# A fused adaLN, long-convolution and SwiGLU kernel on Trainium2: the first block of rows laid out anew

## The chip, the cores and the metric

The kernel runs on one core of one Trainium2 chip (trn2). The metric is the device time in microseconds of one execution; three runs of the kernel before gave a median of 492.25 us (492.23 to 493.86). A separate, profiled execution gives the trace that is read below.

## The reference, cut to what matters

```python
mod = (silu(c) @ w_mod)            # six rows of 576: sa, ca, ga, sb, cb, gb
h = layernorm(q) * (1 + ca) + sa
k_shift[s] = sum over t = 0..3 of k[s - t] * shift_k[:, t]
kv = k_shift * v
y = irfft(rfft(kv padded) * rfft(ssm_k padded))[:2048] + kv * ssm_D
x = q + ga * (h * y)               # a causal long convolution along the 2048 rows, per column
h = layernorm(x) * (1 + cb) + sb
out = x + gb * ((silu(h @ w1) * (h @ w3)) @ w2)
```

There are 2048 rows of 576 columns, the filter ssm_k has 2048 taps for each column, and w1, w3 are 576 x 4608, w2 4608 x 576. All tensors are bf16.

## The kernel before, in words

The rows are cut into eight blocks of 256; partition p of a block's tile holds rows 2p and 2p + 1. The long convolution is done block by block through short Fourier transforms. A block's kv is multiplied by cosine and sine matrices (Fb) on TensorE, which gives its spectrum X; the filter's block of taps, with taps along the partitions (kT), is multiplied by Fk, which gives W, and sums of neighbouring W give V. A block's output spectrum z is the sum of products X[i] V[s - i], in a form with three real products for a complex one; sums and differences of z (real_parts, or for block 0 four instructions in first_block) go through the inverse matrices in Fb. The result is multiplied by hg, the normed and modulated row, and added to x. The second layer norm follows, its rows are turned so that columns lie along the partitions (h2T), and the modulation by cb and sb is applied there as a scale and a bias for each partition (cbcol, sbcol).

The feed-forward part runs over four groups of 512 rows (two blocks each). stream multiplies h2T by chunks of w1 and w3, 512 columns of each per chunk, fetched from memory by SP's queue into wst and into room of the spectra (load_w13); ACT applies silu and copies, DVE multiplies. down multiplies by w2. While group r is streamed, the blocks of group r + 1 are convolved on DVE and ACT, with some matmuls between the streamed ones (conv; conv_second for block 1, beside the first half of stream 0). Group 0 is special: stream(0) begins with the first 256 rows alone, six chunks, as soon as block 0 is turned, and the rows of block 1 follow.

**What sets the order.** All operations are recorded first. Those of setup, early_loads and first_block are fixed: each engine gets them in the order in which they are written. All later ones are put in order by a planner (plan, search): it estimates every operation's time (measure), starts with forty random variations of due times, simulates each and keeps the order with the shortest mean time. It does this at build time, so a change of the fixed part can change the order of all that follows. Every operation is emitted at one line of a helper, so the profile shows L208 for nearly all, and they are told apart by the tiles' names. TensorE's results go to four pairs of PSUM banks (ps), of which the stream uses two. [...]

**Block 0 as it is (first_block, line 1301).** ACT computes the wave matrices by Sin from integer angles (angles, whole_turns, waves; tiles named spectra in the trace, since they lie in that room). shift_taps (846) spreads the four shift taps over all partitions by K = 1 matmuls. load_kv (925) loads k with its three shifted rows beside each pair, five rows of 576 for each partition; kv_rows (1019) forms kv by one product of 6 x 576 and five instructions of 2 x 576 on DVE. load_k (945) loads the taps as they lie, columns along the partitions; k_rows (1052) turns them by ten transposes on TensorE and one copy on ACT. ssm_D is added to tap 0 by two small matmuls, two copies and an addition. cond and mod_piece (869, 882) form the six modulation rows, spread over all partitions, on TensorE; mod_columns (907) forms cb and sb as columns by 60 matmuls. quick_stats (1155) takes a layer norm's statistics on DVE, ln_sums (1130) takes them on ACT. turn_split and turned_split (1262, 1269) turn a half block by six transposes and five evacuations with scale and bias; block 1 is turned by turn_all (1451), ten evacuations' worth in five instructions on ACT.

## Time and profile before

| what | us |
|---|---|
| median of 3 runs (lowest, highest) | 492.25 (492.23, 493.86) |
| profiled execution, its own time | 492.58 |
| its span in the trace | 490.6 |
| PE busy in 0 to 50 us, in 50 to 491 us | 43.44 of 50, 432.34 of 441 |
| DVE busy in 0 to 50 us | 43.21 |
| first matmul of h2T with wst starts at | 33.86 |
| data moved by DMA in the first 60 us | 18.38 MB, 306 GB/s |

The profiled execution's own time is its span and 1.98 us around it. Engines are PE (TensorE), PEld (its weight loads, which overlap), DVE (VectorE), ACT (ScalarE), POOL (GpSimd) and SP (SyncE, which here issues nearly all transfers). A line of the timeline gives the start, the duration, the engine, the operation, the tile written and those read, the shape, how many such instructions were merged, and in brackets how long the engine was idle before and what ended that. The chain of waits is followed back from the last instruction, at each step to what released it. [...] its cost in a row of matmuls is the distance between starts.

### The profile page before, as it was taken

How to read it: one execution, taken by the hardware profiler on the slowest of the kernel's cores; microseconds unless marked ns; L12 is line 12 of the kernel's file. 1: busy time of each engine (PE TensorE's matmuls, PEld its weight loads, DVE VectorE, ACT ScalarE, POOL GpSimd, SP SyncE). 2: the span in 40 equal slices, each digit the busy share in tenths (PEclk: the TensorE clock that was granted, in tenths of full speed). 3: DMA queues.
4: the chain of work that ended last, by engine and by line, in shares of the span. 5: the costliest groups of instructions: out<-in, count | busy, mean ns of one | idle time of the engine just before them, and what ended most of it. 6: DMA issues, size and time to landing. Idle time of an engine off the chain costs nothing.

```text
span 490.6 us, 11215 instructions
## 1 busy us (share of the span) xinstructions
PE 475.8 (97%) x4711; PEld 299.0 (61%) x4712; DVE 338.8 (69%) x450; ACT 285.2 (58%) x559; POOL 28.7 (6%) x41
## 2 busy tenths in 40 slices
PE   6899989998999999999999999999999999999997
PEld 3579879665777444444777444444777444444775
DVE  7988978999995949989776999998941211121012
ACT  5668498855564576778750567887572455555000
POOL 3200000001200000020200000010010000000000
PEclk9999999999999999999999999999999999999999
DMA  8999854665599998469999899764666445360562
GB/s 285 335 341 310 228 159 116 193 203 168 145 199 322 296 322 280 149 189 363 268 275 306 296 271 342 264 181 121 187 169 166 120 139 183 109 207 25 144 170 73
DMA packets 112614, 105.78 MB, mean 216 GB/s; under 512 B 20211, under 2 KB 105140, under 8 KB 112564
## 3 DMA queue, kind: packets, MB, share of 16 engines
q1 hardware_dynamic: 112542, 105.05, 71.9%
q8 instruction: 37, 0.61, 0.5%
q14 instruction: 13, 0.11, 0.1%
q10 hardware_dynamic: 22, 0.01, 0.0%
HBM read 90.10 MB, written 9.44 MB: 203 GB/s over the span
## 4 chain that ended last, share of the span: by engine, by line
PE 85%; DMA 6%; DVE 5%; SPq 1%; ACT 1%; issue 1%; POOL 0%; DVEq 0%; ACTq 0%
PE ps L208 85%; DMA wst<-in_B_w_dram 5%; SPq L208 1%; DVE kv L208 1%; DMA kh<-in_A_k_dram 1%; DVE z L208 1%; DVE bnst L208 1%; DVE hg L208 1%; DVE spectra L208 1%; ACT h2T L208 0%; DMA p<-in_A_shift_k_dram 0%; DVE og L208 0%; DVE p L208 0%; DVE x L208 0%; DVE bnmv L208 0%
## 5 line engine op out<-in xcount | busy, mean ns | idle before, releaser
L208 PE MATMUL ps<-h2T,wst 64*128 64x512 bf16 (+1 forms) x2736 | 277.9, 354 | 0.4 <-DMA wst<-in_B_w_dram 0.3
L208 PEld LDWEIGHTS <-wst 64*128 64x128 bf16 x2736 | 136.6, 94 | 121.9 <-PE ps L208 2.0
L208 PE MATMUL ps<-wst,h 128*128 128x288 bf16 x1152 | 144.1, 286 | 2.3 <-DMA wst<-in_B_w_dram 1.2
L208 PEld LDWEIGHTS <-h 128*128 128x128 bf16 (+2 forms) x1212 | 115.6, 98 | 33.9 <-issue 3.1
L208 ACT ACTIVATE h<-ps 128x512 bf16<-128x512 f32 x144 | 86.4, 600 | 62.5 <-PE ps L208 62.1
L208 ACT CAST u<-ps 128x512 bf16<-128x512 f32 x146 | 84.8, 582 | 56.7 <-PE ps L208 55.6
L208 DVE TENSOR_TENSOR h<-h,u 128x1024 bf16<-128x1024 bf16 x72 | 49.6, 689 | 71.8 <-ACT h L208 42.1
L208 DVE TENSOR_TENSOR p<-spectra 128x3456 bf16<-128x3456 bf16 x28 | 54.7, 1954 | 2.2 <-DMA spectra<-Xd 1.3
L208 DVE TENSOR_TENSOR z<-z,p 128x3456 bf16<-128x3456 bf16 x28 | 54.7, 1953 | 0.3
L208 DVE TENSOR_TENSOR og<-ps,gbrow 128x576 bf16<-128x576 f32 (+1 forms) x18 | 12.4, 690 | 41.7 <-PE ps L208 40.8
L208 ACT ACTIVATE junk<-x 128x576 bf16<-128x576 bf16 x52 | 35.8, 688 | 6.7 <-DVE x L208 6.2
L208 POOL TENSOR_TENSOR lnr<-lnv,neghalf 128x2 f32<-128x2 f32 x13 | 18.7, 1438 | 298.1 <-DVE lnv L208 279.8
L208 DVE TENSOR_TENSOR spectra<-spectra 128x1152 bf16<-128x1152 bf16 (+1 forms) x35 | 25.7, 736 | 2.7 <-ACT spectra L208 2.4
L208 PEld LDWEIGHTS <-Fb 64*128 64x128 bf16 (+1 forms) x250 | 16.0, 95 | 12.2 <-issue 2.2
L208 DVE TENSOR_TENSOR z<-z 128x1152 bf16<-128x1152 bf16 (+1 forms) x30 | 21.1, 710 | 0.1
L208 ACT CAST spectra<-ps 128x576 bf16<-128x576 f32 x32 | 20.4, 652 | 1.0 <-PE ps L208 1.0
L208 ACT ACTIVATE h2row<-x,lnn,lnr 128x64 bf16<-128x64 bf16 (+1 forms) x24 | 13.9, 644 | 10.5 <-DVE lnn L208 7.6
L208 PE MATMUL ps<-kv,Fb 64*128 64x288 bf16 (+1 forms) x142 | 19.3, 283 | 0.1
L208 PE MATMUL ps<-h2T,spectra 64*128 64x256 bf16 x288 | 17.9, 269 | 1.1 <-ACT h2T L208 1.1
L208 DVE TENSOR_TENSOR kv<-kv,p 128x1152 bf16<-128x1152 bf16 x24 | 18.1, 753 | 0.2
L208 PE MATMUL ps<-kT,Fk 64*128 64x288 bf16 (+1 forms) x118 | 17.2, 284 | 0.7 <-ACT kT L208 0.5
L208 PEld LDWEIGHTS <-spectra 64*128 64x128 bf16 x288 | 15.3, 94 | 2.5 <-issue 1.7
(91 smaller groups left out, 262.1 us busy)
## 6 DMA issues: line engine op xcount, KB each, us to landing
wst<-in_B_w_dram SPq DMA_DIRECT2D x72, 512.0 KB, 5.5
wst<-in_B_w_dram SPq DMA_DIRECT2D x72, 288.0 KB, 3.3
kh<-in_A_k_dram SPq DMA_DIRECT2D x7, 720.0 KB, 6.6
wst<-in_B_w_dram SPq DMA_DIRECT2D x72, 64.0 KB, 3.5
spectra<-Xd SPq DMA_DIRECT2D x5, 864.0 KB, 6.1
spectra<-Vd SPq DMA_DIRECT2D x5, 864.0 KB, 6.3
Xd<-spectra SPq DMA_DIRECT2D x4, 864.0 KB, 5.8
Vd<-spectra SPq DMA_DIRECT2D x4, 864.0 KB, 5.9
```

The lines of the kernel that those rows point to most:

```text
L208: getattr(getattr(nc, self.engine), self.method)(*[_real(a) for a in self.args], **{k: _real(v) for k, v in self.kw.items()})
```

## The change

- **Shift taps and kv.** shift_k is loaded to four partitions, and four K = 1 matmul pairs spread it. k of block 0 is loaded once, without shifted rows; DVE forms the products of its rows with each of the four taps, and TensorE adds them up in PSUM with unit matrices shifted by 0, 1 or 2 partitions (views of one tile, moved). DVE multiplies the sum by v.
- **Filter taps of blocks 0 and 1** come through a transposing DMA straight into kT, whose partition p now holds taps p and p + 128; Fk gets other angles for it, with a second pair by a sign, and for blocks 2 on pair_waves computes the former Fk at the start of conv_second. ssm_D enters as a K = 1 term of W's matmuls.
- **Products.** The sums and differences of z for block 0 go into the inverse matrices (Fi, formed on POOL): 12 matmuls for a half block, not 8. V's first part is written straight from PSUM, one half of it by DVE.
- **Rows split.** Row half 0 takes its first statistics on DVE and half 1 on ACT; for the second layer norm it is the other way round. The modulation rows are evacuated by ACT and multiplied by ga in bf16 on DVE.
- **mod_columns** forms the rows by 20 matmuls, copies one partition of each, and turns them by 12 small matmuls.
- **Loads.** w_mod is loaded in five pieces (2, 1, 0, 4, 3); the first chunk of w1 and w3 follows directly.
- **Turning.** Both halves of block 0 are turned after both are normed; three of five evacuations are DVE's. Block 1 is turned in the same way, a half at a time, in outcome. The three warm-up matmuls at the end are dropped, and four are set before shift_taps; all use a tile of zeros as both operands.

The diff, cut; lines taken out of first_block, load_kv, load_k, k_rows and mod_columns stand in the kernel above.

```diff
+        self.angles(nc.vector, 1)
+        self.whole_turns(1)
+        nc.vector.tensor_single_scalar(coli[:, 6:7], coli[:, 6:7], 1, op=ALU.bitwise_and)
+        nc.vector.tensor_copy(self.acol[:, 4:7], coli[:, 4:7])
+        nc.vector.tensor_scalar(self.sign[:], self.acol[:, 6:7], -2.0, 1.0, op0=ALU.mult, op1=ALU.add)
...
+        nc.gpsimd.memset(self.moved[:, 0:2], 0.0)
+        nc.gpsimd.run(lambda: make_identity(self.tc.nc, self.ident), 900.0, (self.ident,))
...
+        self.shk_raw = self.prod.tile([P, D], BF16, name="shk_raw", tag="p")
+        nc.scalar.dma_start(self.shk_raw[0:P:32, :], self.shift_k.rearrange("(q d) j -> q (d j)", q=4))
+        nc.scalar.dma_start(self.drow, self.ssm_D.rearrange("(o n) -> o n", o=1))
+        self.k0 = self.ld.tile([P, 2, D], BF16, name="kh", tag="kh")
+        nc.sync.dma_start(self.k0[:], self.k[0:B, :].rearrange("(p c) d -> p c d", c=2))
+        self.load_taps(0)
+        nc.sync.dma_start(self.crow[:], self.c)
+        self.load_v(0)
+        self.load_mod(2)
+        self.load_mod_tail(0, 3)
+        self.load_x(0)
+        self.load_mod(1)
+        self.load_mod(0)
+        self.load_mod_tail(3, 2)
+        self.load_mod(4)
+        self.load_mod(3)
+        self.load_w13(0, 0)
...
+    def taps_waves(self):
+        self.wave(self.Fk[:, 0:2], self.ang[1][:], 1)
+        self.nc.gpsimd.tensor_scalar(self.Fk[:, 2:4], self.Fk[:, 0:2], self.sign[:, 0:1], 0.0,
+                                     op0=ALU.mult, op1=ALU.add)
...
+    def inverse_sums(self):
+        nc = self.nc
+        for lo, hi, at in ((0, 1, 0), (3, 5, 1)):
+            n = hi - lo
+            nc.gpsimd.tensor_add(self.Fi[:, at:at + n, 0], self.Fb[:, lo:hi, 0], self.Fb[:, lo:hi, 1])
+            nc.gpsimd.tensor_scalar(self.Fi[:, at:at + n, 1], self.Fb[:, lo:hi, 0], -1.0, 0.0,
+                                    op0=ALU.mult, op1=ALU.add)
+    def pair_waves(self):
+        nc = self.nc
+        row = self.lnp.tile([P, P], I32, name="b_row2", tag="junk")
+        ang = self.lnp.tile([P, 2, 2, P], I32, name="ang2", tag="y")
+        nc.gpsimd.iota(row[:], pattern=[[4, P]], base=1, channel_multiplier=0)
+        for x in range(2):
+            for cs in range(2):
+                nc.gpsimd.tensor_scalar(ang[:, x, cs], row[:], self.acol[:, 4 + x:5 + x],
+                                        512.0 * (1 - cs), op0=ALU.mult, op1=ALU.add)
+        nc.vector.tensor_single_scalar(ang[:], ang[:], 2047, op=ALU.bitwise_and)
+        self.wave(self.Fk[:, 0:2], ang[:], 1)
...
+        for q in range(4):
+            at = slice(32 * q, 32 * q + 1)
+                nc.tensor.matmul(ps[:, h, 0:H], self.one[at, :], self.shk_raw[at, h * H:(h + 1) * H],
+                                 start=True, stop=True)
+            src = ps[:, :, 0:H].rearrange("p h (d j) -> p j h d", j=4)
+            dst = self.shk[:, :, 144 * q:144 * (q + 1)].rearrange("p j (h d) -> p j h d", h=2)
+            if q % 2:
...
     def mod_columns(self):
         nc = self.nc
+        rows = self.kvp.tile([1, 2, D], BF16, name="rows", tag="Wo")
+        for i, m in enumerate((4, 3)):
+            p = self.mod_products(m)
+            nc.scalar.copy(rows[:, i, :].rearrange("p (h d) -> p h d", h=2), p[0:1])
+            yield
         ps = self.ps()
+        for i in range(2):
             for j in range(6):
                 lo = min(P * j, 512)
                 n = P if j < 4 else 64
+                out = ps[0:n, i, 4 * j:4 * j + 4] if j < 5 else ps[64:P, i, 16:20]
+                nc.tensor.matmul(out, rows[:, i, lo:lo + n], self.one[0:1, 0:4], start=True, stop=True)
+        nc.scalar.activation(self.cbcol[:], ps[:, 0, 0:20:4], ACT.Copy, bias=1.0)
+        nc.scalar.copy(self.sbcol[:], ps[:, 1, 0:20:4])
...
+    def load_taps(self, s):
+        if s < SPLIT:
+            self.kT = dst = self.kvp.tile([P, 2, D], BF16, name="kT", tag="kT")
         else:
+            dst = self.knat
+        self.nc.sync.dma_start_transpose(dst[:], self.ssm_k[:, B * s:B * (s + 1)])
...
+                ps = self.products([(basis[e][cc][:, cs], rhs[:, cc, :]) for cc in range(2)]
+                                   + [(basis[e][0][0:1, cs], x) for x in more if cs == 0])
+                out = dst(e, cs).rearrange("p (h d) -> p h d", h=2)
+                if more and e + cs == 0:
+                    nc.vector.tensor_copy(out, ps[:, :, 0:H])
+                else:
+                    nc.scalar.copy(out, ps[:, :, 0:H])
...
+            basis = [[self.Fk[:, 2 * e + a] for a in range(2)] for e in range(2)]
+            V = self.V[s] = self.spec.tile([P, 6, D], BF16, name="V", tag="V")
+            yield from self.forward(basis, self.kT,
+                                    lambda e, cs: V[:, 3 * e, :] if s + cs == 0 else W[:, 2 * e + cs, :],
+                                    [self.drow] if s == 0 else [])
...
+    def shifted_rows(self):
+        nc = self.nc
+        p = [self.prod.tile([P, 2, 2, D], BF16, name="p", tag="p"),
+             self.acc.tile([P, 2, 2, D], BF16, name="p2", tag="z1")]
+        for i in range(2):
+            nc.vector.tensor_mul(p[i][:], _ap(self.k0, 0, [[0, 2], [D, 2], [1, D]]),
+                                 _ap(self.shk, 2 * i * D, [[D, 2], [0, 2], [1, D]]))
+        yield
+        ps = [self.ps() for _ in range(2)]
+        for js in ((0, 1), (2, 3)):
+            for c in range(2):
+                for j in js:
+                    at = (c - j) % 2
+                    d = (j - c + at) // 2
+                    for h in range(2):
+                        nc.tensor.matmul(ps[c][:, h, 0:H], self.moved[:, 2 - d:2 - d + P],
+                                         p[j // 2][:, j % 2, at, h * H:(h + 1) * H], start=(j == 0), stop=(j == 3))
+            yield
+        self.kv = kv = self.kvp.tile([P, 2, D], BF16, name="kv", tag="kv")
+        for c in range(2):
+            nc.vector.tensor_mul(kv[:, c, :].rearrange("p (h d) -> p h d", h=2), ps[c][:, :, 0:H],
+                                 self.vt[:, c, :].rearrange("p (h d) -> p h d", h=2))
...
     def first_block(self):
+        blank = self.h2T[0][:, 0, :]
+        self.warm(4, blank)
         self.shift_taps()
         self.whole_turns(0)
+        self.taps_waves()
+        self.forward_waves()
         self.cond_silu()
+        self.inverse_waves()
+        self.warm(6, blank)
+        rows = self.shifted_rows()
+        next(rows)
+        spectrum = self.w_spectrum(0)
+        next(spectrum)
+        next(rows)
+        next(spectrum)
+        next(rows)
+        self.run_all(rows)
         self.cond()
+        self.run_all(spectrum)
+        self.load_taps(1)
+        mean, rstd = self.quick_stats(x1[:, 0, :], "l1")
+        nmr = self.small.tile([P, 1], F32, name="l1nm", tag="nmr2")
+        nc.gpsimd.tensor_mul(nmr[:], mean, rstd)
+        nc.gpsimd.tensor_single_scalar(nmr[:], nmr[:], -1.0, op=ALU.mult)
         self.run_all(self.x_spectrum(0))
+        self.inverse_sums()
         self.run_all(self.v_block(0))
         self.load_kv(1)
         self.load_x(1)
         self.load_w13(1, 1)
         self.load_gb()
         X, V = self.X[0], self.V[0]
         self.accs[0] = z = self.acc.tile([P, 6, D], BF16, name="z0", tag="z0")
+        self.hg[0] = hg = self.lnp.tile([P, 2, D], BF16, name="hg", tag="hg", bufs=2)
+        ssum, ssq = [self.small.tile([P, 1], F32, name="l1" + k, tag=t) for k, t in (("s", "ssum"), ("q", "ssq"))]
+        self.ln_sum(x1, 1, 0, ssum[:])
+        self.ln_sum(x1, 1, 1, ssq[:])
         self.mod_piece(2)
+        nc.vector.tensor_add(X[:, 0, :], X[:, 1, :], X[:, 2, :])
+        nc.vector.tensor_mul(z[:, 0:3, :], X[:, 0:3, :], V[:, 0:3, :])
+        var = self.ln_square(ssum)
+        nc.vector.tensor_add(X[:, 3, :], X[:, 4, :], X[:, 5, :])
+        r = self.ln_rest(ssq, var)
+        nc.scalar.activation(hg[:, 0, :], x1[:, 0, :], ACT.Identity, bias=nmr[:, 0:1], scale=rstd[:, 0:1])
+        nc.vector.tensor_mul(z[:, 3:6, :], X[:, 3:6, :], V[:, 3:6, :])
+        b = self.ln_bias(ssum, r)
+        self.mod_piece(1)
+        nc.scalar.activation(hg[:, 1, :], x1[:, 1, :], ACT.Identity, bias=b[:, 0:1], scale=r[:, 0:1])
         for cc in range(2):
+            nc.vector.tensor_mul(hg[:, cc, :], hg[:, cc, :], self.arow[:])
+        self.mod_piece(0)
+        nc.vector.tensor_add(hg[:], hg[:], _ap(self.brow, 0, [[0, 2], [1, D]]))
+        y = self.lnp.tile([P, 2, D], BF16, name="y", tag="y")
+        ps = []
+        for cc in range(2):
+            terms = []
+            for e in range(2):
+                i = cc * (e + 1)
+                terms += [(self.Fi[:, i, 0], z[:, 3 * e, :]),
+                          (self.Fb[:, i + 2 if i else 0, 1], z[:, 3 * e + 1, :]),
+                          (self.Fi[:, i, 1], z[:, 3 * e + 2, :])]
+            ps.append(self.products(terms))
+        nc.scalar.copy(y[:, 0, :].rearrange("p (h d) -> p h d", h=2), ps[0][:, :, 0:H])
+        nc.vector.tensor_mul(hg[:, 0, :], hg[:, 0, :], y[:, 0, :])
+        nc.vector.tensor_add(x1[:, 0, :], x1[:, 0, :], hg[:, 0, :])
         self.residual_row(0, 1, ps[1])
+        ssum, ssq = [self.small.tile([P, 1], F32, name="l2" + k, tag=t) for k, t in (("s", "ssum"), ("q", "ssq"))]
+        self.ln_sum(x1, 0, 0, ssum[:])
+        self.ln_sum(x1, 0, 1, ssq[:])
+        columns = self.mod_columns()
+        next(columns)
+        var = self.ln_square(ssum)
+        box = []
+        st = self.quick_stats(x1[:, 1, :], "l2", lambda: box.append(self.ln_rest(ssq, var)))
+        r = box.pop()
+        next(columns)
         spectrum = self.w_spectrum(1)
+        next(spectrum)
+        self.run_all(columns)
+        b = self.ln_bias(ssum, r)
+        nc.vector.tensor_scalar(self.h2row[:, 0, 0:D], x1[:, 0, :], r[:, 0:1], b[:, 0:1], op0=ALU.mult, op1=ALU.add)
+        self.normed(0, 1, *st)
+        for cc in range(2):
+            pt = self.turn_split(cc)
+            self.turned_split(pt, cc)
         self.run_all(spectrum)
         self.accs.pop(0)
...
                     yield 1.25
                 for cc in range(2):
                     self.normed(s, cc, *st[cc])
+                    self.turned_split(self.turn_split(cc), 2 * s + cc)
...
-        if s > 1:
-            hT = self.h2T[(s // 2) % 2]
-            for cc in range(2):
-                t = 2 * (s % 2) + cc
-                self.nc.sync.dma_start_transpose(hT[:, :, t * P:(t + 1) * P], self.h2row[:, cc, :])
-            return
-        pt = self.ps((P, 2, 1024), BF16)
-        with self.rec.together():
-            for cc in range(2):
-                self.turn(pt, cc)
-        self.turned(s, pt, 0, 2)
...
     def conv_second(self):
+        self.pair_waves()
```

## The prediction

> **What bounds the kernel now.** I read the page's totals first, then the chain of work that ended last, then the timeline of the first 75 us by engine, then the stretches table there.
>
> ```profile
> PE 475.8 (97%) x4711; PEld 299.0 (61%) x4712; DVE 338.8 (69%) x450; ACT 285.2 (58%) x559; POOL 28.7 (6%) x41
> ```
>
> TensorE is busy 475.8 of 490.6 us, so from the first streamed weights on the end can hardly move except by what PE is given to do. Block 0 is different: there the chain runs along VectorE.
>
> ```profile
> 6.76 1.96 DVE p L208
> 8.72 0.68 DVE kv L208
> ...
> 17.39 1.07 DVE z L208
> ...
> 28.47 0.34 DVE h2row L208
> ...
> 30.98 0.60 DVE h2T L208 x2
> ...
> 64.45 2.39 ACT h2T L208 x5
> ...
> 66.88 49.64 PE ps L208 x682
> ```
>
> From 6.7 to 31 us nearly every piece is one DVE instruction after another. So block 0's DVE list, and what ACT and PE hand it, sets when block 0's rows are turned and the stream of weights can begin:
>
> ```profile
> 32.30 0.60 DVE L208 TENSOR_SCALAR h2T<-ps,cbcol,sbcol 128x128 bf16<-128x128 bf16 x2 [0.73 <-PE ps L208]
> 32.77 1.37 PE L208 MATMUL ps<-wst,u 128*128 128x288 bf16 x9
> 33.86 0.39 PE L208 MATMUL ps<-h2T,wst 64*128 64x256 bf16 x2
> ```
>
> The last of h2T is written at 33.16 (ACT's three, 31.99 + 1.17); the first streamed matmul starts at 33.86, after the last piece of the modulation (mod_piece(5), 32.77). The second bound here is the DMA queue: from 4 to 44 us its share is 0.99 or more in every 2-us stretch. The second and third lines show block 1.
>
> ```profile
> 42.00:44.00 2.00, 2.00 (x40) 2.00 (x37) 1.48 (x3) 1.27 (x3) 0.41 (x1) 1.00 1.12 352
> 60.00:63.00 3.00, 2.91 (x48) 1.89 (x44) 2.54 (x10) 2.18 (x5) 1.37 (x2) 1.00 0.56 111
> 63.00:67.00 4.00, 2.81 (x33) 1.71 (x33) 3.93 (x5) 3.62 (x9) 0.00 (x0) 1.00 0.21 72
> ```
>
> (Columns: stretch, length, busy us of PE, PEld, DVE, ACT, POOL, clock, DMA share, GB/s.) In 63 to 67 us PE is idle 1.19 of 4.00: block 1's turned rows, five ACT instructions in series (2.39 in the chain).
>
> [...] six 512-column warm-ups at 5.66 took 2.72 (0.45 each); at 10.66 sixteen of 288 columns took 2.12 (0.133 each). [...] the trace has 688 ns for 576 elements and 2.27 us for four in a row. [...] the trace has only the 128-element angles (2.48 us for six).
>
> **The change, part by part.** I lay the new program order on each engine with durations from the rows before.
>
> *Start and taps.* DVE loses kh's memset (0.78) and takes h2T's from POOL (0.53 there): constants to 1.9, four angles (0.9), one whole_turns (0.43), three tiny ones, to 3.6. PE's four warm-ups now start at about 1.65 and end at 3.4. The shift taps' four copies of 576 replace three of 1024/256; at 1.2 ns an element (1.22 for 1024) 0.70 each on DVE, about 0.65 on ACT; q0, q2 end at 5.7 on DVE, q3 on ACT at 6.15. DVE: whole_turns(0), now 768 wide, 0.62 to 1.05, take 0.7: 6.4. ACT: Fk, Fb, silu and inverse waves follow, to 9.55; the sign product on POOL costs 0.41 to 1.0 and ends near 7.9, hidden (wanted at 11).
>
> *Row sums.* Removed from DVE: 1.96 + 0.75 + 3 x 0.76 + 0.76 = 5.8 us (6.76 to 12.56). Added: two products of 2304 elements, 1.96 x 2304/3456 = 1.31 each, so 6.4 to 9.0; a PSUM copy of the first tap spectrum 0.70; two PSUM products of 0.75. PE adds 16 shift matmuls, 16 x 0.133 = 2.1, of which only the last eight (from 9.4, to 10.45) lie between. kv ends at 11.6: **1.0 earlier**.
>
> *Taps by transposing DMA.* Removed: 10 transposes (1.27) and an ACT copy (1.12), once per block; the drow columns and their copies. Added: four K=1 matmuls (0.5, PE has room) and SP's issue of a transpose: the trace has 1.55 and 1.30 against 1.05 for the two loads. Landing is 3.3 after issue with the queue free at 60 us, so 4.5 at best here; I take 6.5, before W's first product at 7.0. SP's queue behind it (c, v, the w_mod pieces) slips 0.5; c is wanted first, at 7.9, and landed 3 to 4 us after issue before. The second transpose waits for kT's readers (12.1)[...].
>
> *Spectra and products.* PE: cond, the last two W products and x_spectrum end at 14.2. ACT's four copies of X (2.27) end at 15.4 (16.37 before). DVE: one quick_stats (1.16) instead of two (2.32), no V copy (0.39), and of z only two sums (0.45) and two products (1.06): four of 0.47 = 1.9 are gone, for 8 more PE matmuls (24 for 16, +1.1) and Fi on POOL (four small two- and one-input operations, 1.5 to 2.5, by 16.5, hidden until 18.4). DVE would end z at 17.6, but waits for x1's row-1 sums, now on ACT (2 x 0.82 after 15.4 = 17.1): z ends at **18.4** (21.9 before).
>
> *Gate.* ACT becomes the chain: ga 17.75, hg row 0 18.5, arow 19.1, hg row 1 19.85, brow 20.45. DVE after it: 0.46 + 0.76, hg ready 21.7. Inverse on PE 18.4 to 21.6, y on ACT 21.05. Row 0: 0.46 + 0.46 = 22.6; row 1: 0.75 + 0.46 = 23.85 (28.47 before): **4.6 earlier**.
>
> *Statistics, columns, turn.* ACT: row 0's sums 24.3, two one-row copies 25.5, W copy 26.1, cbcol and sbcol 26.5. DVE: both h2row by 26.45 (31.07 before). mod_columns falls from 60 matmuls (4.44) to 20 of 0.14 and 12 small: 3.7, in PE's wait from 21.6 to 26.1. Turning: per half three DVE (0.30) beside two ACT (0.39), so 26.6 to 28.4. The last 12 matmuls of W(1) (1.6), before in gaps at 28.09 and 29.57, now stand behind the transposes, 27.2 to 29.0, since PSUM pairs come free only at 27.5 and 28.4. **First streamed matmul 29.0**, 4.9 earlier than 33.86.
>
> *What is given back.* mod_piece(5), ten full matmuls (1.37 at 32.77), stood ahead of the stream; its weights landed near 31.8 by the landing marks, so it now lies inside the stream: +1.4. Gain 3.5.
>
> *Weights.* The third chunk's last half is issued at 30.05 and, at the 8.0 us to landing of such 512 KB pieces, is there at about 38; PE first used it at 40.98, 7.1 after the stream began. After: wanted at 29.0 + 1.4 + 7.1 = 37.5. Bytes ahead fall by 0.43 MB (k's shifted copy: 1.3 us at 335 GB/s), while two transposes in a full queue cost 0 to 1.3 more each (the queue fell to 168 and 133 GB/s around the one at 46.80): landing 36.7 to 39.3, a wait of 0 to 1.8; I take **+0.3**.
>
> *Block 1.* DVE is full from 33 to 44 and nearly so to 62, so block 1's h2row moves with it, -4.5, but pair_waves puts 0.43 (the 512-wide row) on DVE, 0.72 on ACT and 2.5 on POOL there. Turning takes 1.8 on DVE and ACT together for the ACT series of 2.4, half of it before row 1 is normed. DVE side: about 60.5; PE, with its own work, 60.3. PE's idle 1.2 shrinks to about 0.3: **-0.9**.
>
> *After that* the same program follows; its order is searched anew by the planner, which I count at nothing, +-1.5 (the weights' waits it left before: 0.68 at 144.78, 0.53 at 247.21, 0.27 at 442.52).
>
> Sum: -4.9 + 1.4 + 0.3 - 0.9 = -4.1. On the profiled execution (span 490.6, 1.98 around it, 492.58) that is 488.5; its time is 0.33 above the median shown, 492.25, against which I forecast 488.1.
>
> **Rivals.** *A: the taps land late.* PE takes in order, and W's first product stands ahead of the shift sums; if the transpose lands at 9 rather than 6.5, kv and all behind it slip 2.0, giving 490.1. For: the queue is full from 2 us on. Against: only k lies ahead of it. *B: DMA decides.* Transposes block the queue fully (2.7 instead of 1.4 us each) and the third and fourth chunks wait; the stream's start is worth only what DMA came earlier, +1.8, giving 489.9. Against: the bytes fell. *C: the gain is whole.* PE hides mod_piece(5) in its remaining waits (-1.0) and turning ends at 28.0 (-0.8): 486.3. *D: slower.* The order searched anew issues weights too late at the changes from stream to block: a piece issued only when PE asks for it costs its whole landing, 6.4 (the chain's piece at 436.07, which is covered now). It decides once more than 4.1 + 2.5 = 6.6 us are lost, so from the second such piece: 492.25 - 4.1 + 12.8 = 501. For: the chain holds four such landings, and the planner's start times all move. Against: PE waited only 0.27 to 0.68 at them, and the later program is the same.
>
> **How the numbers follow.** Forecast 0.50 (486.6 to 489.6); C 0.17; A 0.13; B 0.12; D 0.08. About 0.5% (2.5 us) is what a measurement tells from no change, so the line lies at 489.8. Faster: 0.48 + 0.17 + 0.06 + 0.06 = 0.77; within: 0.02 + 0.07 + 0.06 = 0.15; slower 0.08. The range leaves out D and the far tail of C: 485.6 to 491.0.
>
> **What would show it.** kv ends near 11.6 on DVE; z near 18.4; the chain from 15 to 21 runs on ACT, not DVE; both h2row by 26.5; first matmul of h2T with wst near 29; PE idle at block 1's turn below 0.5. Wrong if W's first product waits for the transposing DMA past 7.5, if PE waits for the third chunk by over 1 us, or if PE's idle after 70 us grows by more than 1.5.

## The result and the profile after

| | before | after |
|---|---|---|
| median (lowest, highest), 14 runs each | 492.49 (491.76, 494.69) | 495.03 (493.63, 497.47) |
| after to before, 95% interval | | 1.0047 [1.003, 1.0064] |
| profiled execution, its span | 490.6 | 492.9 |
| first matmul of h2T with wst | 33.86 | 32.24 |
| PE idle after 70 us | 3.40 | 5.53 |

The change made the kernel slower by 0.47%, where 0.8% faster was forecast. The totals and two rows of the groups, from the page of after (total, mean ns, then idle before it):

```profile
PE 478.3 (97%) x4685; PEld 296.7 (60%) x4685; DVE 337.0 (68%) x453; ACT 289.2 (59%) x564; POOL 41.7 (8%) x49
...
L208 POOL TENSOR_TENSOR lnr<-lnv,neghalf 128x2 f32<-128x2 f32 x13 | 24.5, 1886 | 296.7 <-DVE lnv L208 296.7
...
L208 PE MATMUL ps<-h2T,spectra 64*128 64x256 bf16 x288 | 17.7, 269 | 1.4 <-DVE h2T L208 1.0
```

PE has 26 matmuls fewer than before and is busy 2.5 us longer, 2.3 of that in the first 28 us (24.73 busy, 22.45 before), where much of its work runs at half clock. POOL is busy 13 us longer. The chain of waits in block 0 (start, length, what):

```profile
3.87 0.69 PE ps L208 x8
4.56 0.75 DVE shk L208
5.31 0.04 issue
5.35 5.99 PE ps L208 x28
11.36 1.42 DVE kv L208 x2
...
16.07 3.79 POOL Wo L208 x4
19.85 0.56 POOL rstd L208
20.43 0.17 DVE nmr L208
20.63 0.87 ACT hg L208
...
29.26 11.96 PE ps L208 x141
```

The long DVE pieces of before (p 1.96, z 1.07) are gone from it. In their place stand PE (6 us up to kv) and POOL: the tile Wo holds the new inverse matrices Fi. PE up to kv, from the timeline (moved holds the shifted unit matrices; p and z are the products with the four taps, the second pair of which lies in z's room):

```profile
5.35 2.72 PE L208 MATMUL ps<-h2T 128*128 128x512 bf16 x6 [0.80 <-DVE shk L208]
7.86 1.05 PE L208 MATMUL ps<-kT,Fk 128*128 128x288 bf16 x4
...
9.19 1.15 PE L208 MATMUL ps<-p,moved 128*128 128x288 bf16 x8
10.18 0.65 PE L208 MATMUL ps<-kT,Fk 128*128 128x288 bf16 x4
10.67 1.14 PE L208 MATMUL ps<-z,moved 128*128 128x288 bf16 x8
```

The six warm-ups and the four matmuls of W's first piece start 0.43 and 0.24 us apart; from 8.84 us on, matmuls of 288 columns start 0.12 apart, at full clock. (One such matmul lasts 0.28 in the trace, the last of the sixteen at 13.68, so what it costs in a row is read from the starts. The clock column of the profile reads 1.00 in these first microseconds all the same; half clock at the start is read from the starts.) The end of block 0 on PE:

```profile
26.62 0.37 PE L208 MATMUL ps<-one,Wo 1*128 1x4 bf16 x6 [0.22 <-DVE bnst L208]
27.15 0.37 PE L208 MATMUL ps<-one,Wo 1*128 1x4 bf16 x6 [0.16 <-ACT Wo L208]
27.63 1.24 PE L208 MATMUL ps<-moved,h2row 128*128 128x128 bf16 x12
29.26 3.04 PE L208 MATMUL ps<-kT,Fk 128*128 128x288 bf16 x12 [0.39 <-ACT h2T L208]
32.24 1.94 PE L208 MATMUL ps<-h2T,wst 64*128 64x256 bf16 x30
```

h2T was complete at 30.22, but W(1)'s last twelve matmuls stood ahead of the stream and took 3.04 us, 0.24 from start to start; at full clock such a matmul takes 0.12. The stretches (the last three columns are clock, DMA share, GB/s) say so, and show block 1's turn below:

```profile
28.00:30.00 2.00, 1.61 (x14) 0.98 (x13) 1.52 (x7) 1.51 (x4) 1.43 (x4) 0.78 1.09 388
30.00:32.00 2.00, 2.00 (x10) 1.15 (x8) 2.00 (x2) 1.26 (x2) 0.00 (x0) 0.50 1.09 366
32.00:34.00 2.00, 2.00 (x32) 1.51 (x32) 2.00 (x4) 1.65 (x5) 0.00 (x0) 0.86 1.09 378
...
60.00:63.00 3.00, 2.93 (x48) 1.96 (x42) 2.01 (x8) 1.55 (x3) 1.48 (x2) 1.00 0.88 352
63.00:67.00 4.00, 2.62 (x41) 2.30 (x42) 4.00 (x9) 3.94 (x11) 0.00 (x0) 1.00 0.43 88
```

In 28 to 34 us, (0.22 + 0.50 + 0.14) x 2 = 1.72 us of clock were lost. In 63 to 67 PE is idle 1.38 us, where before it was 1.19: the new turning did not shorten it.

Followed by the stream's n-th matmul, after leads by 1.62 us at the first, trails by 0.16 at the 288th (52 us), is about level (0.08 behind) at the 433rd (65 us), and trails by 2.5 at the last. So in this pair of profiles what block 0 gained is gone by 52 us, and the rest is lost late. In a second pair (e17 and e12 below, the same two kernels) it leads by 2.3, 0.6 and 0.7 at these places and trails by 1.0 at the last.

### The profile page after: what moved, and what is told of

It reads as the page before. It is cut to its first block, busy times and chain, and to the rows that moved or that the text cites. A ratio compares the mean times of both kernels' runs of the same rounds, so it can differ in the third digit from the quotient of the medians.

```text
span 492.9 us, 11167 instructions
## 1 busy us (share of the span) xinstructions
PE 478.3 (97%) x4685; PEld 296.7 (60%) x4685; DVE 337.0 (68%) x453; ACT 289.2 (59%) x564; POOL 41.7 (8%) x49
## 4 chain that ended last, share of the span: by engine, by line
PE 75%; DVE 11%; POOL 5%; DMA 4%; ACT 3%; issue 1%; SPq 0%; POOLq 0%; ACTq 0%; DVEq 0%
PE ps L208 75%; POOL lnr L208 3%; DVE z L208 3%; DMA wst<-in_B_w_dram 2%; DVE p L208 2%; ACT junk L208 1%; DVE hg L208 1%; DVE h L208 1%; DMA kT<-knat 1%; POOL Wo L208 1%; DVE x L208 1%; DVE kv L208 1%; DMA p<-in_A_shift_k_dram 1%; DVE bnst L208 1%; ACT h L208 0%
## 5 line engine op out<-in xcount | busy, mean ns | idle before, releaser
L208 PEld LDWEIGHTS <-wst 64*128 64x128 bf16 x2736 | 135.0, 94 | 123.7 <-PE ps L208 2.1
L208 PEld LDWEIGHTS <-h 128*128 128x128 bf16 x1152 | 112.4, 98 | 31.8 <-issue 3.4
L208 ACT ACTIVATE junk<-x 128x576 bf16<-128x576 bf16 x56 | 38.4, 686 | 19.1 <-DVE x L208 18.5
L208 POOL TENSOR_TENSOR lnr<-lnv,neghalf 128x2 f32<-128x2 f32 x13 | 24.5, 1886 | 296.7 <-DVE lnv L208 296.7
L208 PEld LDWEIGHTS <-Fb 64*128 64x128 bf16 (+1 forms) x234 | 14.8, 95 | 12.3 <-DVE z L208 3.5
L208 ACT ACTIVATE h2row<-x,lnn,lnr 128x576 bf16<-128x576 bf16 (+1 forms) x24 | 14.0, 644 | 12.8 <-DMA h2T<-h2row 9.7
L208 PE MATMUL ps<-kT,Fk 64*128 64x288 bf16 (+1 forms) x120 | 19.5, 304 | 1.5 <-DMA kT<-knat 1.1
L208 DVE TENSOR_TENSOR z<-z 128x1152 bf16<-128x1152 bf16 x26 | 19.5, 751 | 0.1
L208 PE MATMUL ps<-kv,Fb 64*128 64x288 bf16 (+1 forms) x134 | 17.9, 284 | 0.2
L208 DVE TENSOR_TENSOR z<-spectra 128x3456 bf16<-128x3456 bf16 (+1 forms) x9 | 15.9, 1763 | 0.0
```

What stands on the lines that cost most here:

```text
L208: getattr(getattr(nc, self.engine), self.method)(*[_real(a) for a in self.args], **{k: _real(v) for k, v in self.kw.items()})
```

## The experiments

**Theory.** (a) Block 0 gains 1.6 and not 4.9 because its new path runs on PE, which is at half clock up to 8.8 us and again from 29.1 to 32.5, and because POOL's Fi sums hold a power that DVE waits for (a power: POOL raises a layer norm's variance to -1/2). (b) The new order of the later part puts POOL's powers, z and loads where PE waits for them. **Rivals:** the weights decide, so the start of the stream is worth nothing; the later order as such costs the time; the clock falls by itself.

In all experiments but e12 and e17 the order of everything behind block 0 is the list that the planner gave for after, kept, except where an edit moves something. Ratios are to the kernel before run beside them (35 to 62 executions; 9 to 22 of the experiment), with 95% intervals.

### One mend at a time

**e1**: the consumer of the slowest power is moved up on DVE. The timeline of after, and the group's row of e1:

```profile
335.46 13.67 POOL L208 TENSOR_TENSOR lnr<-lnv,neghalf 128x2 f32<-128x2 f32 x1 [82.06 <-DVE lnv L208]
```
```profile
L270 POOL TENSOR_TENSOR lnr<-lnv,neghalf 128x2 f32<-128x2 f32 x13 | 11.8, 913 | 311.8 <-DVE lnv L270 311.8
```

DVE's list by the tiles it writes, in words:

```diff
-  DVE: lnv, z, kv, z, p, kv, z, h, p, h, z, z, h, spectra, lnn
+  DVE: lnv, z, lnn, kv, z, p, kv, z, h, p, h, z, z, h, spectra
```

> The order of the kernel after is kept; only one small DVE instruction (lnn of the layer norm near 335 us) is moved up, right behind the sum product that follows lnv, so that DVE waits there for POOL's power lnr. Theory (the power is starved by gapless two-input work on DVE): DVE is idle 0.4 to 1.0 us near 336, the power ends in 0.7 to 1.6 us instead of 13.7, the two DVE waits of 0.58 at 349 and 351 and PE's wait of 0.81 us for z at 360 vanish; 0.5 to 1.2 us less than after, about 494.1. Rival (the new order as such, its DVE list and its loads, costs the late part): PE's wait at 360 stays over 0.5, the time stays at 495.0 within 0.4. Rival (POOL was slow for another reason): the power still takes over 5 us, DVE waits that long for it, and the time rises by 1 or more.

The power fell from 13.67 to 1.05 us for a DVE pause of 0.58; PE's wait at 360 fell from 0.81 to 0.45. Ratio 1.003 [1.001, 1.005]. In both kernels this power ended some 0.55 us behind the last two-input product that DVE issued without a gap: that DVE held it up is shown. It is worth about 0.4 us on PE, less than I expected; lnn stood 13 us down DVE's list anyway.

**e2**: two pieces of W(1) at 23 us, a third at 27.

```diff
+        spectrum = self.w_spectrum(1)      # behind the copy of y
+        next(spectrum)
+        next(spectrum)
```

> The order of everything after block 0 is kept. In block 0, two of W(1)'s four pieces are put right behind block 0's inverse (about 23 us), the third ahead of the last small matmuls of mod_columns; only the fourth stays behind the turning. Theory (the stream starts late because W(1) stands ahead of it at half clock[...]): the spacing of the turning's transposes falls from 0.10 towards 0.055, the first streamed matmul comes at 29.8 to 30.8 instead of 32.24, and the whole is 1.2 to 2.2 us shorter than after: 492.8 to 493.8. Rival (weights decide, so the start of the stream is worth nothing): the stream starts as early, but PE then waits for the second or third chunk, and the time stays at 495.0 within 0.5. Rival (the copies of W on ACT stand ahead of what the turning needs): h2T is done later than 30.2 and the start gains under 0.7.

Ratio 1.0083 [1.0054, 1.0112]. The third rival came out, by way of the PSUM pairs: the turning needs all four, and a piece kept one of them:

```profile
30.43 0.27 PE L270 MATMUL ps<-moved,h2row 128*128 128x128 bf16 x2 [0.67 <-ACT h2T L270]
30.68 0.96 PE L270 MATMUL ps<-kT,Fk 128*128 128x288 bf16 x4
32.67 3.60 PE L270 MATMUL ps<-h2T,wst 64*128 64x256 bf16 x32 [1.04 <-ACT W L270]
```

The stream's first pair was that of the last piece, so it waited for ACT's copy. (kv came at 13.66 here, so the start of 32.67 is to be set beside e1's, with kv at 13.77: 31.82.) Two stretches of half clock followed, 6.8 and 3.4 us long. Later edits rename pairs.

**e3**: matmuls without a purpose ahead of the small ones at 27.

```diff
+            for _ in range(2):
+                nc.tensor.matmul(ps[:, i, 128:512], busy[:, 0:P], busy, start=True, stop=True)
```

> The order of everything is kept; four matmuls of 384 columns that compute nothing are put ahead of the two groups of small matmuls at 26.6 and 27.15 us, into a part of the same PSUM tile that nobody reads. Theory (clock): transposes at 0.055 to 0.08 spacing instead of 0.10, the twelve W(1) matmuls in 1.5 to 2.2 us instead of 3.04, the first streamed matmul at 30.4 to 31.4; 0.8 to 1.8 us shorter than after. Rival (clock is not it, the pieces of W(1) wait for PSUM pairs and ACT's copies): W(1) still takes 2.7 to 3.1 us, nothing gained, up to 0.3 lost. Rival (weights): start earlier, no shorter.

Ratio 1.0022 [1.0005, 1.0039]. W(1) took 1.6 us, but it did so in e1 too, which has no such matmuls: this run can't tell. Instead both lost 1.7 us of clock at 64 to 70, behind the gap at block 1's turn. The stretches of e1:

```profile
64.00:66.00 2.00, 1.40 (x21) 1.30 (x22) 2.00 (x5) 1.94 (x7) 0.00 (x0) 0.84 0.37 83
66.00:68.00 2.00, 2.00 (x22) 1.64 (x19) 1.97 (x4) 0.73 (x2) 0.00 (x0) 0.50 0.00 0
68.00:70.00 2.00, 1.99 (x29) 1.70 (x25) 1.93 (x3) 0.75 (x2) 0.00 (x0) 0.81 0.94 340
```

**e4**: POOL's Fi sums right behind the inverse waves.

```diff
         self.inverse_waves()
+        self.inverse_sums()
```

> The order of everything is kept; POOL's four instructions for the inverse matrices (Fi) are issued right behind the inverse waves instead of behind X's spectrum. Theory (they hold the power of row 1's statistics, for which DVE waits 0.85 us and ACT 0.63 at 20.4): that wait goes, hg is ready 0.5 to 0.9 earlier (22.4 to 22.8), both h2row likewise, and the first streamed matmul comes 0.4 to 0.9 earlier; 0.4 to 0.9 us shorter than after. Rival (the PE side sets the rows, by the inverse and the columns): hg is earlier but h2T is done within 0.2 of 30.2, and nothing is gained. Rival (POOL's instructions, now beside DVE's long products at 9 to 12, slow DVE there): kv ends later than 12.78.

Ratio 1.0003 [0.9986, 1.0019]. In the timeline of POOL in after, then in e4:

```profile
16.03 0.60 POOL L208 TENSOR_TENSOR Wo<-Fb 128x128 bf16<-128x128 bf16 x1
16.61 1.10 POOL L208 TENSOR_SCALAR Wo<-Fb 128x128 bf16<-128x128 bf16 x1
17.67 0.93 POOL L208 TENSOR_TENSOR Wo<-Fb 128x256 bf16<-128x256 bf16 x1
18.57 1.28 POOL L208 TENSOR_SCALAR Wo<-Fb 128x256 bf16<-128x256 bf16 x1
19.82 0.58 POOL L208 TENSOR_TENSOR rstd<-var,neghalf 128x1 f32<-128x1 f32 x1
```
```profile
9.39 0.42 POOL L270 TENSOR_TENSOR Wo<-Fb 128x128 bf16<-128x128 bf16 x1
9.79 0.30 POOL L270 TENSOR_SCALAR Wo<-Fb 128x128 bf16<-128x128 bf16 x1
10.06 0.67 POOL L270 TENSOR_TENSOR Wo<-Fb 128x256 bf16<-128x256 bf16 x1
10.70 0.41 POOL L270 TENSOR_SCALAR Wo<-Fb 128x256 bf16<-128x256 bf16 x1
```

The same four take 1.8 us where DVE has no two-input product and 3.9 beside such products. hg came 0.51 earlier (22.80) with kv 0.13 later. The third rival is out: kv moved no more. The medians fell by 0.44% against after, 2.2 us, more than the 0.4 to 0.9 expected; part of that is half clock further on, which fewer of its executions met (table below).

### Half clock

**e5, e10**: the long PE gaps at 63 and 119 us filled with matmuls that compute nothing; e5 puts those at block 1's turn into the pair being evacuated, e10 four of them into the pair freed before.

In words:

```diff
+   behind block 1's last transposes: 4 x matmul(pair[:, 1, 0:512], Fb, Fb)   # e5: one more, earlier
+   behind block 2's X: 18 x matmul(pair[:, 0 or 1, 288:512], Fb, Fb)
```

> The kernel after in its own order; only matmuls that compute nothing are added where its PE waits longest once the stream runs: one and four of 512 columns around block 1's last transposes (gaps of 0.34 and 1.04 us at 63 to 65), eighteen of 224 columns ahead of block 2's inverse (gap of 2.08 us at 119). Theory (a PE gap of about 1 us or more is followed by some 3.4 us at half clock in most executions, each costing 1.7 us): no stretch of half clock in 60 to 130 us in the profile, and the median 1 to 3 us below after's (ratio to before 0.999 to 1.003 instead of 1.0047), the spread of its runs smaller. Rival (the clock falls for reasons of its own[...]): half clock in 60 to 130 as often as before, no gain or a loss of 0.2 to 0.5 for the work added. Rival (what PE waits for is DVE and ACT, and they are slower for the added traffic): gaps end later by over 0.3.

> The fill run showed no half clock but its matmuls at block 1's turn stood in the PSUM pair that DVE then evacuated, and cost 0.87 us there. Here the four are put into the other pair, freed before. Theory (clock): no half clock from 35 to 130 us in the profile, block 1's PE gap filled and not followed by delay, and a median 0.5 to 1.0 us below the fill run: ratio to before 1.001 to 1.003. Rival (half clock is not what parts the medians): as the fill run, 1.0036, or above.

Ratios 1.0036 [1.0022, 1.0049] and 1.0022 [1.0007, 1.0036]; no half clock in either profile. In e5, DVE waited 0.78 us for the fillers before it emptied the pair at 64.62, which cost 0.87. The medians' fall lies within the overlap of the intervals.

The eleven profiles with these gaps unfilled (after twice, e1 to e4, e6, e7, e9, e13, e15) have 14 windows of half clock after 20 us (late windows), each 3.4 us long and costing 1.7: five at 28 to 36 us (two of them end to end in e2), five behind block 1's turn, two behind the gap at 119, two behind waits of 2.4 us for a load. The six profiles with them filled (e5, e8, e10, e11, e14, e16) have none; the two of before have 0 and 1. In the kernels with after's layout each follows a gap of 0.7 us or more, or the thin work at 26 to 29; the one of before follows sixty matmuls of 64 columns, without a gap.

One profile for each kernel is little, and the executions that were timed say more. Each has its mean clock on record. In the profiled executions of after and the experiments one such window went with 0.995 to 0.997, two with 0.993, three (e2) with 0.99, none with 0.999 or 1.0; I count 0.992 as two and 0.998 as none.

| kernel | executions | with a late window | with two or more |
|---|---|---|---|
| before, beside all experiments | 262 | 135 | 17 |
| after, e17 | 32 | 27 | 4 |
| e1, e2, e3, e6 | 75 | 67 | 15 |
| e4 (POOL's sums early) | 22 | 10 | 4 |
| e5, e10 (late gaps filled) | 44 | 35 | 0 |
| e7, then e8 (the same with fillers) | 14, 14 | 7, 0 | 1, 0 |
| e9, then e11 (with mends and fillers) | 22, 14 | 5, 4 | 0, 0 |
| e13, then e14 (the same) | 22, 14 | 11, 5 | 0, 0 |
| e15, then e16 (the same) | 22, 22 | 17, 2 | 2, 0 |

So e5 and e10 did not remove late half clock: their profiles were among the few executions without it. From e7 to e8, which differ in the fillers only, it went, so it isn't the clock's own doing alone; but e9 has little of it and fills nothing late, and e11, which adds fillers to it, has no less. Filling is not what decides it alone, and where in an execution the window lies isn't on record.

**e6**: z ahead of hg on DVE at 117.

```diff
-  DVE: z, hg, h, z, spectra
+  DVE: z, z, hg, h, spectra
```

> The kernel after in its own order, but for one DVE instruction: the sum of z that block 2's first inverse waits for at 119 us is put ahead of the sum of hg (0.75 us) and a product of the stream (0.69). Theory (this wait of 2.08 us comes from the new order's place of z on DVE): PE's gap there falls to 0.6 to 1.0, and the time falls by 1.0 to 1.4, and by up to 1.7 more where a half-clock stretch followed that gap. Rival (PE next waits for h of the stream instead): the gap only moves to the down matmuls behind it, and under 0.4 is gained.

Ratio 1.0031 [1.0015, 1.0046]. The gap fell from 2.08 to 0.94, with 0.59 new at the second inverse; its gain was lost in the profile to a wait of 2.40 for a chunk of w2 at 264.65 us. That wait was 0.47 in after, 2.19 in e4, 0.26 in e5, with the same order of issue on SP, a load of V (864 KB) just ahead of the chunk: it differs from profile to profile, and why isn't shown.

### When PE reaches full clock

In one kernel's two profiles kv's end follows the start of 0.12 spacing on PE, which I call full clock: 8.8 us and kv 12.78 (after), 11.3 and 14.06 (e17). **e9** takes W's second piece and four warm-ups out of the way of the shift matmuls; **e13** also fills the early gaps, but for 0.4 at 6.5 us; **e15** fills that too.

```diff
-        self.warm(6, blank)
+        self.warm(2, blank)                # e15: 4
...
         next(spectrum)
         next(rows)
-        next(spectrum)
         next(rows)
         self.run_all(rows)
+        next(spectrum)
...
-        self.warm(4, blank)                # e13 and e15 only
+        self.warm(5, blank)                # e15: 6
...
+            for i in range(4 if q == 3 else 0):
+                nc.tensor.matmul(ps[:, i % 2, H:512], self.h2T[0][:, 0, 0:P],
+                                 self.h2T[0][:, 0, 0:512 - H], start=True, stop=True)
```

> The kernel after in its own order, with only PE's order at 5 to 12 us changed: two 512-column warm-ups in place of six ahead of the first piece of W, both groups of shift matmuls directly behind that piece, and W's second piece and cond behind them (the PSUM pairs of what follows are renamed). Theory (kv came at 12.8 and not 11.6 because PE, at half clock, stood behind warm-ups and behind W's second piece): kv ends at 11.2 to 12.0, z at 18.0 to 18.9 and the first streamed matmul 0.7 to 1.5 earlier than in an after with the same clock (32.24 there, 31.8 in the runs without half clock at 29); ratio to before 1.000 to 1.003. Rival (kv is earlier but z waits for W's copies on ACT or for the modulation rows on PE): kv under 12.0, z still above 19.2, nothing gained.

> The shift-first kernel with PE kept busy from its first matmul on: five warm-ups ahead, not four, and four of 224 columns that compute nothing in the last taps' PSUM tile ahead of its copy, so that the gaps at 3.5 and 4.6 us are filled. In all profiles so far kv's end followed the moment at which PE's matmuls reached full clock (8.84 us: kv 12.78; 10.97: 13.82; in the shift-first order 10.88: 12.62; 12.52: 13.04). Theory [...]: full clock by 8.5 us, kv at 11.2 to 12.0, z at 18.2 to 19.2, first streamed matmul at 29.6 to 30.5; ratio to before 0.997 to 1.001. Rival (full clock comes at a time of its own): full clock at 9 to 12.5 as before, kv at 12.4 or later, as in the shift-first run.

> The no-early-gap kernel still had gaps of 0.1 at 3.9 us and 0.4 at 6.5 us, and reached full clock only at 12.4. Here six warm-ups ahead (not five) and four behind the taps (not two) close both, so that PE works without a gap of over 0.1 us from 1.57 us on. Theory as it stands now [...]: full clock by 8.5 us, kv at 11.3 to 12.2, first streamed matmul 0.8 to 1.6 earlier than the 31.96 of the no-early-gap run; ratio to before 0.997 to 1.001. Rival (the clock comes up by itself, or matmuls of zeros and of one row do not count): full clock at 9 to 12.5 again, kv above 12.4.

> The kernel after unchanged, beside the others, for a second profile. Theory: the moment of full clock, the place of the half-clock stretch and the loads' waits differ from those of its first profile although nothing was changed (full clock at 8.6 to 12.4, kv at 12.7 to 14.0, one or more stretches of half clock after 28 us), while the power of 13.7 us behind DVE comes again within 0.1; ratio to before 1.003 to 1.006. Rival (the profile of a kernel repeats): full clock again at 8.8, half clock at 29.

e9: 1.0005 [0.9988, 1.0022], full clock at 10.9, kv 12.62, later than either side had it. e13: 1.0004 [0.9986, 1.0022], full clock at 12.9, kv 13.39: full clock by 8.5, expected from filling the gaps at 3.5 and 4.6, did not come. e15: 0.9994 [0.998, 1.0009], full clock at 7.4, kv 11.53; its first streamed matmul, 31.36, came 0.6 earlier than e13's, less than expected, with half clock at 28. e17: 1.0046 [1.0026, 1.0067], and its power of 13.67 us came again; its profile has no half clock after 20 us. PE in e13, then in e15:

```profile
6.92 1.14 PE L270 MATMUL ps<-kT,Fk 128*128 128x288 bf16 x4 [0.40 <-ACT Fk L270]
7.99 0.66 PE L270 MATMUL ps<-knat,Fk 1*128 1x288 bf16 x2
8.58 2.10 PE L270 MATMUL ps<-p,moved 128*128 128x288 bf16 x8
10.47 2.12 PE L270 MATMUL ps<-z,moved 128*128 128x288 bf16 x8
```
```profile
7.41 0.68 PE L270 MATMUL ps<-kT,Fk 128*128 128x288 bf16 x4
8.03 0.41 PE L270 MATMUL ps<-knat,Fk 1*128 1x288 bf16 x2
8.37 1.15 PE L270 MATMUL ps<-p,moved 128*128 128x288 bf16 x8
9.42 1.14 PE L270 MATMUL ps<-z,moved 128*128 128x288 bf16 x8
```

Without the gaps of 0.4 and 0.14 us full clock came 5 us sooner. Two further profiles with the same early fillers agree: e14, with the gap of 0.4, has full clock at 12.9 and kv 13.46; e16, without it, 5.2 and 11.52. From the end of the last gap of over 0.1 us ahead of full clock to full clock the runs took, in us: after 3.5 (5.35 to 8.84), e9 5.3, e17 5.8, e14 5.9, e13 6.0, e11 7.1; from PE's first matmul at 1.57, e16 3.6, e15 5.8. So it came 3.5 to 7.1 us behind the last gap, in the same kernel once 3.5 and once 5.8 (after and e17), once 3.6 and once 5.8 with the same gapless start (e16 and e15). What sets the moment within this range, no run shows.

### Together

**e7, e8, e11, e14, e16** add the mends: e4, e1 and e6 in all; e7 has other early warm-ups (they waited for ACT's copy, 1.26 us) and e3's; e8 adds fillers; e11 is e9 with fillers; e14 is e13 and e16 is e15 with the same. Their diffs are made of those above.

> All mends together, the rest in the order of after: Fi's sums early, POOL's consumer next, z ahead of hg, ten short warm-up matmuls in the last taps' PSUM tile in place of six long ones that wait for a pair (and five ahead, not four), one warm-up of 384 columns ahead of each group of small matmuls at 27, and PSUM pairs renamed so that the stream's first pair is not the one of W(1). Theory (the head is bound by PE's gaps and half clock and by POOL's sums): kv done at 11.0 to 12.3 instead of 12.78, W(1)'s last twelve matmuls at full clock, first streamed matmul at 28.8 to 30.3, and the time 3 to 5 us below after: ratio to before 0.994 to 0.998. Rival (weights): PE waits for the second or third chunk, and the ratio stays above 0.999. Rival (each gain is taken back at block 1's turn, which DVE and ACT set): the first 65 us gain under 0.5.

> The combined kernel with the filling matmuls of the fill run (five instead of eighteen at block 2's inverse, where its gap should be shorter). Theory (clock): no half clock after 35 us, median 0.5 to 2 us below the combined kernel, the least spread of all. Rival (clock falls on its own): no difference from the combined kernel, or up to 0.5 slower.

> PE's early order of the shift-first run, Fi's sums early, POOL's consumer next, z ahead of hg, and fillers at block 1's turn (in the freed pair) and seven short ones at block 2's inverse. Theory: the gains add up: first streamed matmul at 29.0 to 30.3, no half clock after 35, ratio to before 0.994 to 0.999. Rival (what is gained in the head is lost behind it, to weights that land when they land or to block 1's DVE work): the stream starts by 30.3, but its lead over after is below 0.7 us at 100 us.

> The second combined kernel with PE kept busy early. Theory: full clock by 8.5 us, kv under 12.0, first streamed matmul at 28.8 to 30.0, no half clock after 35 us, PE idle after 70 us 2.5 to 3.5; ratio to before 0.993 to 0.998. Rival (the head's gain is used up behind it): the first matmul by 30.0 and still a ratio above 0.999.

> The third combined kernel with the gapless start. Theory: full clock by 8.5 us, kv 11.3 to 12.2, first streamed matmul at 29.3 to 30.6; PE idle after 70 us 2.5 to 5.0, since the waits for loads there differ from run to run; ratio to before 0.993 to 0.999. Rival (the head's gain does not reach the end): started by 30.6 and a ratio of 0.999 or above.

| run | ratio | kv | first stream matmul | PE idle after 70 us |
|---|---|---|---|---|
| e7 | 1.001 [0.9986, 1.0035] | 12.93 | 30.71 | 3.29 |
| e8 | 1.0002 [0.998, 1.0023] | 12.96 | 30.75 | 3.70 |
| e11 | 1.0003 [0.9979, 1.0026] | 13.04 | 31.31 | 2.94 |
| e14 | 1.0008 [0.9982, 1.0033] | 13.46 | 31.70 | 5.02 |
| e16 | **0.9981 [0.9966, 0.9997]** | 11.52 | 29.42 | 2.83 |

e16 (median 491.43) is 0.19% faster than before, with an interval that just leaves out no change; it is the last of five combinations and was timed beside before once. Part of its lead is less late half clock: among executions without any, its median is 491.35 and that of before beside it 492.34. Of the five it alone kept within its expectation. e7, e11 and e14 missed theirs, and so did e8: without a late window in any execution its median is not below e7's (493.96, 493.63), so what the fillers saved in clock does not show in the time.

The chain of waits of e16 in block 0 (the helper's line is 270 in the experiments; z is here the second tap product):

```profile
8.01 1.36 DVE z L270
9.37 0.04 issue
9.41 17.50 PE ps L270 x139
...
27.00 0.81 ACT h2T L270 x2
...
27.86 4.24 PE ps L270 x57
```

With POOL out of the way, block 0 from 9.4 us on is nearly all PE. **e12**, the kernel before again:

> The kernel before unchanged, for a second profile of it. Theory (its PE gaps, 1.57 and 0.89 us in block 0, three of 0.3 to 0.5 at 65 us with work between, 0.7 and 0.84 at 117, lead to half clock seldom or late): none or one stretch of half clock, PE idle after 70 us 3.0 to 4.5. Rival (it falls as often as in after): two or more stretches, and the first profile was lucky.

Full clock came 1 us later than in its first profile (its last three warm-ups took 1.48 us, not 0.87), and there was one window of half clock, 27.9 to 31.3; kv ended at 12.30 all the same, since before forms it on DVE. PE idle after 70 us: 4.19.

## Why the prediction was wrong

| the forecast's step | forecast | after | e16 |
|---|---|---|---|
| kv ends | 11.6 | 12.78 | 11.52 |
| z ends | 18.4 | 19.59 | 18.55 |
| hg ready | 21.7 | 23.31 | 21.90 |
| both h2row | 26.45 | 28.13 | 26.73 |
| h2T done | 28.4 | 30.22 | 28.82 |
| first streamed matmul | 29.0 | 32.24 | 29.42 |

The data flow was read rightly: e16, the same layout with these causes mended and with warm-ups and fillers that the forecast did not have, keeps the forecast within 0.45 us at every step. What failed:

- **"PE adds 16 shift matmuls, 16 x 0.133 = 2.1, of which only the last eight (from 9.4, to 10.45) lie between."** and **"kv ends at 11.6."** The last eight ran at full clock in after and took no longer than forecast, but started at 10.67 and not at 9.4, because of what stood ahead of them on PE, which the forecast priced at nothing or at full clock: six warm-ups at half clock held PE from 5.35 to 7.86 (W's first product was put at 7.0), W's first piece, mostly at half clock, took 1.33 us up to 9.19, against 0.96 in e15, and W's second piece, 0.49, stood between the two groups of shifts. In e17 the first eight ran partly at half clock too and held PE for 1.70 us, where they held it for 0.99 in after. The row 0.133 came from 10.66 us of before. This is the first failed step: 1.2 us at kv, 2.5 in e17; with PE at full clock by 7.4 us and the order changed, kv came at 11.53 (e15).
- **"Fi on POOL (four small two- and one-input operations, 1.5 to 2.5, by 16.5, hidden until 18.4)."** It took 3.9 us, to 19.85, and the power of row 1's statistics was queued behind it: DVE idle 0.85. By POOL's six angle instructions of before (2.48, 128 elements each) the 768 elements here come to 2.5, an estimate, and e4 took 1.8 without two-input DVE products beside it. I named what Fi feeds, not what stands behind it on POOL.
- **"The last 12 matmuls of W(1) (1.6)... 27.2 to 29.0."** 3.04 us at half clock in the first profile, 1.6 in e17. PE had only matmuls of 4 and 128 columns from 26.6 to 28.9, with gaps, where before had W(1) between its transposes. Whether this thin work lets the clock fall is not shown: e3 put warm-ups there and can't tell.
- **"Block 1... -0.9."** PE's idle time in 60 to 70 us went from 1.28 to 1.84; the forecast had some 0.3 left at the turn.
- **"its order is searched anew by the planner, which I count at nothing, +-1.5"**: PE idle after 70 us was 5.53 and 5.51 in after against 3.40 and 4.19: 1.3 to 2.1 lost, to z at 119 (2.08 for 0.70 + 0.84), to z at 360 (0.81, new), the rest to loads. The forecast's own sign of being wrong, growth by more than 1.5, was met in the first pair of profiles and not in the second.

Right were, near enough, **mod_piece(5)** (+1.4; the lead shrank by 1.65 from the first to the 288th matmul in e16) and, within its size, the **weights**: PE did not wait for the third chunk, in after or in e16, so rival B is out. Rival A is out too: W's first product did not wait for the taps. D came out in sign, but not by its mechanism: no load cost PE over 2.4 us in any profile.

The sum for e16: -4.4 at the start, +1.65, block 1 +0.1 (its fillers included), then +0.9: -1.8 at the last streamed matmul of its profile, against -4.1. So the forecast overrated block 1's turn by 1.0 and left out what the later order gives back.

**What stays open.** By the recorded clocks, e17 had 0.89 late windows an execution and before beside it 0.60: at 1.7 us each that is an estimated 0.5 of the 2.5 us between the medians. At an equal number of windows after stays slower: without one, 494.14 (4 executions) against 492.34 (27); with one, 495.50 (12) against 493.45 (23). So about 2 us are left for the start, the later order and the loads, and the record does not part these. No run put the later order of before behind the new block 0, so what the order costs is read from PE's idle time in two pairs of profiles alone. The medians of single mends do not add up either (e4 -0.44%, e9 -0.42%, e11 with both still -0.44%, each known to some 0.2 to 0.3%).

## What to carry to other kernels

Before moving work from DVE to PE at the start of a kernel, ask at what clock PE will be there: price it at the half-clock spacing (here 0.24 us for 288 columns, against 0.12) unless PE has been busy without a gap for some 7 us (full clock came 3.5 to 7.1 us behind the last gap here), count the warm-ups themselves as work that stands ahead on PE, and fill gaps with cheap matmuls in a PSUM pair that nobody waits for. For every step put on POOL, list what is queued behind it, and price it beside a DVE that issues two-input products (the four Fi sums took 3.9 us beside them and 1.8 without). Before a trace's missing half clock is put down to an edit, look at the clock of all executions. And where a model that knows neither searches the later order anew, count what that may lose, here 1.3 to 2.1 us of PE.

## What the runs showed of the hardware

- A POOL power of 128 x 2 took 0.69 us beside an idle DVE (132.21 in after) and 13.67 beside 13.4 us of gapless two-input DVE products, in all eleven profiles of this order without e1's mend (13.68 in e4); there it ended 0.55 us behind the last of 13 DVE instructions, and not between any two of them. In e1, with a DVE pause behind the first, it took 1.05. It isn't always so: at 121.96 us of after a power took 2.40 us, ending 0.56 behind one DVE product (1.84) while the next one ran. What decides it, no run shows.
- One-input POOL work was slower there too: 128 x 256 bf16 took 0.41 us in e4, without such products, and 1.28 beside them in after. Fk's sign product (128 x 512), where I had put at most 1.0, took 2.96 and ended 0.48 us behind DVE's two long products.
- Two profiles of the same kernel (after and e17) differ by 2.5 us in the start of full clock, by 1.3 at kv and by a window of half clock (1.7 us); one profile is not enough to size a step of 1 us at the start.
- Half clock followed the gap of 1.04 us at block 1's turn in five of the eleven profiles that have it, and that of 2.08 us at 119 in two of nine, with PE busy on both sides, so not behind each such pause. Each of the 14 late windows lasted 3.4 us, two of them end to end (6.8, e2).
